# One of the seven block products of layer two's mixing taken as seven smaller ones, with the block sums kept in DRAM

## The chip, the cores and the metric

The kernel runs on one core of a Trainium2 chip. The metric is device time in microseconds (us) for one execution of the whole program: the median of several runs. Profile times are from one profiled execution, counted from the start of its span. The engines are called as the profile calls them: PE (TensorE; PEld is its weight load), DVE (VectorE), ACT (ScalarE), POOL (GpSimd) and SP (SyncE, which issues most DMAs).

## What is computed

Two layers, each a linear-attention block and a mixer block, on 2048 tokens of width 512, all in float32:

```python
def _B_ref(x, w_in, w_sp, b_sp, w_out):
    Fh = F // 2                                   # 896
    z = _gelu(jnp.einsum("bsd,df->bsf", x, w_in))
    z1 = z[..., :Fh]
    z2 = _layernorm(z[..., Fh:], axis=-1)
    g = jnp.einsum("ts,bsf->btf", w_sp, z2) + b_sp[None, :, None]
    return jnp.einsum("bsf,fd->bsd", z1 * g, w_out)

x = A_x
x = x + _A_ref(_layernorm(x, axis=-1), A_wqkv, A_wo)
x = x + _B_ref(_layernorm(x, axis=-1), B_w_in, B_w_sp, B_b_sp, B_w_out)
x = x + _A_ref(_layernorm(x, axis=-1), A_wqkv, A_wo)
x = x + _B_ref(_layernorm(x, axis=-1), B_w_in, B_w_sp, B_b_sp, B_w_out)
```

The weights of both layers are the same arrays. The einsum with `w_sp` (2048 x 2048 times 2048 x 896) is the *mixing*. The change is in the second layer's mixing.

## The kernel before

**Precision.** Every float32 matrix product is made of three: each operand is split into a high part (ScalarE's copy to float32r, `high`, L101) and a low part (VectorE's subtraction, `low`, L104), and TensorE adds high x high, high x low and low x high (`mm3`, L115 to L117; in the mixing L1111 to L1113). So every operand passes through ScalarE and then VectorE before TensorE can use it.

**Order.** The schedule is written out by hand: the order of the calls in the source is the order on each engine's queue, and each queue runs in order. Buffers are numbered slots that are taken and given back in turn: 22 pages of 128x512 (`pg`), 6 quads of 128x2048 (`qd`), 4 big ones (`bg`), and the 8 banks of PSUM. Whoever takes a slot waits until its last user is done.

**Stages of a layer.** (1) Attention, `P1` and `transition`. (2) The projection stage, `P2.run`: a loop over s = 1 to 18, over token blocks of 128. At step s it makes block s - 1's attention output (`c`, 12 matmuls, and `c2`, VectorE's addition to x, L644), its statistics (L222, L224, then three small POOL operations) and its normalised copy (ScalarE, L235), turns that copy by a round through DRAM (`xturn`, VectorE's L286), splits it (`d_high`, `d_low`, L101 and L104 into a `qd`) for block s - 2, multiplies block s - 3 by the second half of `w_in` (`e`, 24 matmuls of 448 columns, deadline of `d_low`), and takes one or two pieces of the first half (`f`, 12 matmuls each). Before `c` it turns and splits the attention operand of block s (`b_high`, `b_low`). The Gelus that empty the banks run on ScalarE (L702, L727). In layer two (`seven` is true) the last 1024 tokens of `f` are made by seven block products (`side`, `tail`), with sums of `w_in` that `Make` made in layer one's output stage and keeps in DRAM (`kept`; POOL's queue fetches them, L774). (3) The mixing, `P4.run`: `w_sp` and z2 are cut in 2 x 2 blocks and multiplied with seven block products instead of eight, in `ORDER`: P4, P2, P1, P6, P7, P5, P3. The tokens are 16 blocks, so each product has 8 steps of 24 or 18 matmuls of 128x512. The sums of `w_sp` blocks that four of the products need were made in layer one by POOL (`Sums`) and are kept in DRAM (`s`). At step g the loop prepares the weights of g + 2 and the z operand of g + 3 (`prepare`: L1070, L1075 on ScalarE, L1077, L1081 on VectorE), issues the matmuls of g (`mm`), and fetches the weights of g + 4 (`fetch`). After a product's last step `evac` adds its banks into `gb`. P2 and P1 of the mixing share the two banks `delta`, which P1 empties. (4) The output stage, in the same `run`: 16 blocks of 21 matmuls with `w_out` (`o`, `zsplit` two blocks ahead, x loaded two blocks ahead, L1212 the addition).

Of the kernel before, what the change touches and what calls it, by code (L numbers as in the profile page):

```python
# [10 lines left out]
F32 = mybir.dt.float32  # L11
# [42 lines left out]
def mixer_kernel(ctx: ExitStack, tc: tile.TileContext, x_in, wqkv, wo_d, win1_d, win2_d, wsp_d, bsp_d, wout_d,  # L54
# [514 lines left out]
    class P2:  # L569
# [309 lines left out]
        def run(self, sums):  # L879
            w1 = self.win1  # L880
            for s in range(1, NT + 3):
                self.loadx(s + 1)
                self.qturn.load(s + 1)
                if s in self.qturn.by_pe:
                    self.c(s - 1)
                    self.b_high(s)
                    self.c2(s - 1)
                    self.b_low(s)
                    self.c_stats(s - 1)
                    if s >= 2:  # L890
# [115 lines left out]
                self.done = [a22, a11, a12]  # L1006


    class P4:


# [2 lines left out]
        WITH3 = ("P4", "P2", "P1", "P5")  # L1014
        H1, H3, H2 = slice(0, 384), slice(384, 512), slice(512, 896)

        def __init__(self, p2, sums):
            self.L = p2.L
            self.p2, self.sums = p2, sums
            self.raw, self.w, self.z, self.z1, self.x, self.zs = {}, {}, {}, {}, {}, {}  # L1020
            self.steps = [(p, k) for p in self.ORDER for k in range(HT)]
            self.beta = self.delta = None
            self.ready, self.loaded = deque(), []
            self.wout = {}

        def fetch(self, g):
            if g >= len(self.steps):
                return
            p, k = self.steps[g]
            t = quads.get([P, 2, 512])  # L1030
            if p in ("P1", "P2", "P4"):
# [32 lines left out]
        def prepare(self, gw, gz):  # L1064

            gw, gz = (g if g is not None and g < len(self.steps) else None for g in (gw, gz))
            if gw is not None:
                r = self.raw.pop(gw)
                w = self.w[gw] = quads.get([P, 2, 2, 512], F32R)
                nc.scalar.activation(w[:, 0], r, AF.Copy)  # L1070
            if gz is not None:
                n = 512 if self.steps[gz][0] in self.WITH3 else 384
                z, sign, t = self.operand(gz)
                h, l = pages.get(PAGE, F32R), pages.get(PAGE, F32R)
                nc.scalar.activation(h[:, 0:n], z, AF.Copy, scale=sign)  # L1075
            if gw is not None:
                nc.vector.tensor_sub(w[:, 1], r, w[:, 0].bitcast(F32))  # L1077
                quads.put(r)
            if gz is not None:
# [7 lines left out]
                self.z[gz] = (h, l)  # L1087

        def mm(self, g):
            p, k = self.steps[g]  # L1090
            h, l = self.z.pop(g)
            w = self.w.pop(g)
            first, last = k == 0, k == HT - 1
            if p in ("P4", "P2", "P5") and first:
                self.delta = [banks.get(PAGE) for _ in range(2)]
            if p in ("P4", "P2", "P1", "P5") and first:
                self.beta = [[banks.get(PAGE) for _ in range(3)] for _ in range(2)]
            if p in self.WITH3:
                for j in range(2):
                    self.acc(self.delta[j], h, l, self.H3, w, j, first and p != "P1",  # L1100
                             last and p != "P2")
# [13 lines left out]
        def unit(self, n, f):  # L1115
            return self.gb[n][:, f, :]
# [24 lines left out]
        def evac(self, p):  # L1141
# [3 lines left out]
            if p in ("P4", "P1", "P5"):  # L1145
                for j in range(2):
                    n = 2 + j if p == "P1" else j
                    V.tensor_add(self.unit(n, 3), self.delta[j], self.unit(n, 3) if p == "P5" else bs[n])
# [70 lines left out]
        def run(self, nxt):  # L1219
# [14 lines left out]
            for g in range(n):  # L1234
# [17 lines left out]
                if k == HT - 1:  # L1252
                    self.evac(p)
            pages.put(*self.bs)
            self.zsplit(1)
# [1 line left out]
            for i in range(NT):  # L1257
                self.loadx(i + 2)
                self.gates()
                if i == NT - 1 and nxt is not None:  # L1260
                    nxt.T(1)
                self.o(i)
                self.zsplit(i + 2)
                if make is not None:
                    make.step(i)
                if nxt is not None:
                    self.join(i, nxt)

# [16 lines left out]
                nxt.T(0)  # L1285

    sums = Sums()
    p1 = P1(0)
    p1.start()
    for L in range(2):  # L1290
# [41 lines left out]
```

## Time and profile before

| what | value |
|---|---|
| median of 3 runs | 1388.9 us (1388.66 to 1390.36) |
| the profiled execution's own time | 1389.01 us |
| its span | 1387.2 us, 17681 instructions |
| PE busy | 1380.8 us, 100%, 6232 matmuls |
| DVE busy | 911.5 us, 66% |
| ACT, POOL busy | 594.3 us (43%), 432.5 us (31%) |
| DMA | 235.67 MB, mean 170 GB/s; 52.4% of 16 engines in the hardware queues, 0.8% in POOL's |

How to read it: the share of busy time is an average over stages. A matmul's listed duration includes the time in which it overlaps with its neighbours; the distance of starts tells what one costs. In a timeline a row has start, duration, engine, line, operation, output<-inputs, and in brackets the idle time before it and what ended that. In this execution layer two's projection stage lies at about 836 to 1020 us, its mixing from 1036 to 1311 us, and layer one's output stage around 620 to 700 us.

### The profile page before, as it was taken

The numbers are of one execution on the slowest core, as the hardware profiler recorded it, in microseconds if no ns is written. First come the engines' busy times: TensorE is split into PE (matmuls) and PEld (weight loads), VectorE is DVE, ScalarE is ACT, GpSimd is POOL, SyncE is SP. The second block draws the span as 40 slices with busy tenths as digits, with TensorE's granted clock in tenths as the row PEclk, the third lists the DMA queues.
The fourth block names the chain that finished last, engine by engine and source line by source line (L and its number), as shares of the span: only waits on it lengthen the run. The fifth ranks groups of instructions, "written<-read, shape, count | busy, mean of one in ns | idle before, by whom it ended". The sixth has DMA issues, their size and how long they took to land.

```text
span 1387.2 us, 17681 instructions
## 1 busy us (share of the span) xinstructions
PE 1380.8 (100%) x6232; PEld 1157.8 (83%) x6232; DVE 911.5 (66%) x1314; ACT 594.3 (43%) x918; POOL 432.5 (31%) x514
## 2 busy tenths in 40 slices
PE   9999999999999999999999999999999999999998
PEld 7888888888888888888888888888888888888887
DVE  6776887753756597676667768866766345776642
ACT  6674543334442234241357655444454432342410
POOL 3343454443135451432023425522220000233310
PEclk9999999999999999999999999999999999999999
DMA  5541367866678974356845415555364324544442
GB/s 172 174 129 62 118 186 229 258 207 212 217 242 287 296 236 134 126 205 229 279 130 162 128 46 152 175 175 162 120 212 148 103 91 129 175 129 159 167 145 91
DMA packets 151145, 235.67 MB, mean 170 GB/s; under 512 B 12560, under 2 KB 56592, under 8 KB 151056
## 3 DMA queue, kind: packets, MB, share of 16 engines
q1 hardware_dynamic: 147456, 228.11, 51.3%
q0 software_dynamic: 1728, 3.15, 0.8%
q10 hardware_dynamic: 1872, 3.28, 0.6%
q8 instruction: 49, 0.80, 0.2%
q14 instruction: 40, 0.33, 0.1%
HBM read 162.40 MB, written 72.09 MB: 169 GB/s over the span
## 4 chain that ended last, share of the span: by engine, by line
PE 99%; DMA 0%; DVE 0%; POOL 0%; ACT 0%; issue 0%; DVEq 0%
PE bank L117 19%; PE bank L115 19%; PE bank L116 19%; PE bank L1112 13%; PE bank L1113 13%; PE bank L1111 13%; PE bank L793 1%; PE bank L794 1%; PE bank L792 1%; PE bank L247 1%; DMA pg<-in_x_dram 0%; DVE st L222 0%; ACT pg L101 0%; POOL rs L227 0%; DVE pg L237 0%; PE bank L516 0%
## 5 line engine op out<-in xcount | busy, mean ns | idle before, releaser
L1112 PE MATMUL bank<-qd,pg 128*128 128x512 f32 x800 | 311.3, 389 | 0.0
L1111 PE MATMUL bank<-qd,pg 128*128 128x512 f32 x800 | 311.2, 389 | 0.0
L1113 PE MATMUL bank<-qd,pg 128*128 128x512 f32 x800 | 311.2, 389 | 0.0
L1077 DVE TENSOR_TENSOR qd<-qd,qd 128x1024 fp32r<-128x1024 f32 x112 | 160.4, 1432 | 143.5 <-ACT qd L1070 143.0
L1070 ACT ACTIVATE qd<-qd 128x1024 fp32r<-128x1024 f32 x112 | 118.6, 1059 | 241.4 <-DMA qd<-s 109.6
L1133 POOL TENSOR_TENSOR bg<-bg,pg 128x512 f32<-128x512 f32 x56 | 81.4, 1458 | 320.8 <-DMA pg<-z 294.9
L1112 PEld LDWEIGHTS bank<-qd,pg 128*128 128x128 f32 x800 | 150.2, 188 | 31.5 <-DVE qd L1077 0.4
L1111 PEld LDWEIGHTS bank<-qd,pg 128*128 128x128 f32 x800 | 150.2, 188 | 31.4
L1113 PEld LDWEIGHTS bank<-qd,pg 128*128 128x128 f32 x800 | 150.2, 188 | 31.0
L117 PE MATMUL bank<-qd,pg 128*128 128x512 f32 x384 | 149.9, 390 | 0.0
L226 POOL TENSOR_SCALAR rs<-mv 128x1 f32<-128x1 f32 x96 | 39.1, 407 | 332.7 <-DVE mv L224 332.4
L986 POOL TENSOR_TENSOR pg<-pg,pg 128x512 f32<-128x512 f32 x64 | 92.5, 1445 | 91.0 <-DMA pg<-in_wsp_dram 65.1
L235 ACT ACTIVATE pg<-pg,nb,rs 128x512 f32<-128x512 f32 x63 | 51.1, 811 | 145.7 <-POOL nb L229 145.4
L115 PE MATMUL bank<-qd,pg 128*128 128x512 f32 x288 | 112.4, 390 | 0.1
L116 PE MATMUL bank<-qd,pg 128*128 128x512 f32 x288 | 112.1, 389 | 0.0
L115 PE MATMUL bank<-bg,qd 128*128 128x448 f32 x256 | 94.0, 367 | 0.0
L116 PE MATMUL bank<-bg,qd 128*128 128x448 f32 x256 | 93.6, 366 | 0.0
L117 PE MATMUL bank<-bg,qd 128*128 128x448 f32 x256 | 93.4, 365 | 0.0
L101 ACT ACTIVATE pg<-pg 128x512 fp32r<-128x512 f32 (+1 forms) x87 | 53.5, 615 | 81.2 <-DVE pg L286 38.0
L286 DVE STREAM_TRANSPOSE pg<-pg 128x512 f32<-128x512 f32 x79 | 85.1, 1077 | 4.5 <-DMA pg<-yt 1.7
L115 PE MATMUL bank<-wo,qd 128*128 128x512 f32 x224 | 87.1, 389 | 0.0
L116 PE MATMUL bank<-wo,qd 128*128 128x512 f32 x224 | 87.1, 389 | 0.0
(157 smaller groups left out, 2683.2 us busy)
## 6 DMA issues: line engine op xcount, KB each, us to landing
qd<-s SPq DMA_DIRECT2D x64, 512.0 KB, 3.4
qd<-in_wsp_dram SPq DMA_DIRECT2D x48, 512.0 KB, 4.3
pg<-in_wsp_dram SPq DMA_DIRECT2D x64, 256.0 KB, 4.9
s<-pg SPq DMA_DIRECT2D x64, 256.0 KB, 4.8
pg<-x SPq DMA_DIRECT2D x64, 256.0 KB, 3.3
pg<-z SPq DMA_DIRECT2D x56, 256.0 KB, 3.8
x<-pg SPq DMA_DIRECT2D x48, 256.0 KB, 2.9
z<-pg SPq DMA_DIRECT2D x44, 256.0 KB, 2.1
```

The source lines that it names most:

```text
L101: nc.scalar.activation(h, src, AF.Copy)
L115: nc.tensor.matmul(out, ah, bh, start=start, stop=False)
L116: nc.tensor.matmul(out, ah, bl, start=False, stop=False)
L117: nc.tensor.matmul(out, al, bh, start=False, stop=stop)
L286: nc.vector.transpose(y.rearrange("p c (t m) -> p m c t", m=4), r.rearrange("p (m c j) -> p m c j", m=4, c=4))
L986: nc.gpsimd.tensor_tensor(t, a, b, op=OP.add)
L1070: nc.scalar.activation(w[:, 0], r, AF.Copy)
L1077: nc.vector.tensor_sub(w[:, 1], r, w[:, 0].bitcast(F32))
L1111: m(out, h[:, o], w[:, 0, j, :], start=start, stop=False, skip_group_check=True)
L1112: m(out, h[:, o], w[:, 1, j, :], start=False, stop=False, skip_group_check=True)
L1113: m(out, l[:, o], w[:, 0, j, :], start=False, stop=stop, skip_group_check=True)
L1133: nc.gpsimd.tensor_tensor(u, u, z1, op=OP.mult)
```

## The change

In layer two's mixing, the product P2 (blocks a = `w_sp` rows of the third and fourth quarter, columns of the second half; z operand the second half of the tokens, first 512 features) is itself cut in 2 x 2 blocks and taken with seven products, in the order `NEST`. Its 8 steps of 24 matmuls become 14 steps ("N", two to a product) of 12 matmuls of 128x512. Three of the seven use blocks of `w_sp` that are loaded and split as before; four use sums, which a new class `Inner` makes once, splits, and keeps in DRAM as ready high and low parts; POOL's queue fetches these, 1 MB for a step. `Inner` makes 16 sums, each a *unit*: one addition or subtraction on VectorE, a high part on ScalarE, a low part on VectorE, and in the next unit two stores of 256 KB by SP. Four units run in layer one's output stage, twelve in layer two's projection stage. The z operands need sums as well (`token_sums`, in P4's steps; four pages held until P5). The inner products gather in banks X (two, over P1, P6, P7, P4, read out after each) and Y (two, for P2, P3, P5 each), and are added into `gb` on VectorE after each. Since the 128 features of `delta` are now done with the others, P1 of the outer product starts its own `delta` bank and adds into `gb`.

The core of the diff:

```diff
@@ P2.run
                 if self.seven:
                     self.side(s)
+                    if s == 5:
+                        inner.begin(3)
+                    elif 6 <= s < 16:
+                        for _ in range(2 if 10 <= s < 13 else 1):
+                            inner.unit()
...
+    class Inner:
+        def __init__(self):
+            self.d = {m: dram.tile([2, P, 2, 2, 512], F32, name=f"n{m}") for m in range(1, 5)}
...
+        def store(self):
+            for m, k, n, p in self.made:
+                nc.sync.dma_start(self.d[m][k // 2][:, k % 2, n, :], p.bitcast(F32))
+                pages.put(p)
+            self.made = []
+
+        def unit(self):
+            self.store()
+            if not self.todo:
+                return
+            k, u = self.todo.popleft()
+            if u == 0:
+                self.S1 = t = self.raw.pop("22")
+                nc.vector.tensor_add(t, self.raw["21"], t)
+            elif u == 1:
+                t = self.raw.pop("21")
+                nc.vector.tensor_sub(t, self.raw["11"], t)
...
+            h, l = pages.get(PAGE, F32R), pages.get(PAGE, F32R)
+            split(h, l, t)
...
+            if self.left:
+                self.fetch()
+                self.left -= 1
...
     class P4:
+        NEST = ("P1", "P6", "P2", "P7", "P3", "P4", "P5")
+        OWN = {"P1": (2, 8), "P2": (2, 12), "P4": (3, 12)}
+        SUM = {"P3": 4, "P5": 1, "P6": 2, "P7": 3}
...
+            for p in self.ORDER:
+                if p == "P2" and self.nested:
+                    self.steps += [("N", d) for d in range(14)]
+                else:
+                    self.steps += [(p, k) for k in range(HT)]
...
     def fetch(self, g):
+            if p == "N" and self.NEST[k // 2] in self.SUM:
+                self.w[g] = quads.get([P, 2, 2, 512], F32R)
+                nc.gpsimd.dma_start(self.w[g], inner.d[self.SUM[self.NEST[k // 2]]][k % 2])
+                return
...
+        def token_sums(self, k):
+            q, o = divmod(k, 2)
+            if o == 0:
+                self.T2[q], self.T3[q] = pages.get([P, 2, 256]), pages.get([P, 2, 256])
+            a, b = ztile[8 + k], ztile[12 + k]
+            nc.vector.tensor_sub(self.T3[q][:, o], b[:, 256:512], a[:, 256:512])
+            nc.vector.tensor_add(self.T2[q][:, o], self.T3[q][:, o], a[:, 0:256])
...
+        def nested_mm(self, g):
...
+            for i in range(2):
+                f = slice(i * P, (i + 1) * P)
+                for o in range(2):
+                    first, last = q == 0 and o == 0, q == 1 and o == 1
+                    m(out[i], h[:, o, f], w[:, o, 0], start=first and (own or name == "P1"), stop=False,
+                      skip_group_check=True)
+                    m(out[i], h[:, o, f], w[:, o, 1], start=False, stop=False, skip_group_check=True)
+                    m(out[i], l[:, o, f], w[:, o, 0], start=False, stop=last and (own or name == "P4"),
+                      skip_group_check=True)
...
+                if name == "P1":
+                    V.tensor_add(u[1], self.X[i], bs[2])
+                elif name == "P6":
+                    V.tensor_add(u[2], self.X[i], bs[2])
+                elif name == "P2":
+                    V.tensor_add(u[1], u[1], self.Y[i])
...
@@ P4.run
+                if self.nested and 1 <= g < 5:
+                    self.token_sums(g - 1)
...
                 if make is not None:
                     make.step(i)
+                    if i < 5:
+                        inner.unit() if i else inner.begin(1)
+                    elif i == 5:
+                        inner.store()
```

More of the change, by code (lines that the diff above doesn't have):

```diff
@@ L1020, in __init__ @@
             self.raw, self.w, self.z, self.z1, self.x, self.zs = {}, {}, {}, {}, {}, {}
-            self.steps = [(p, k) for p in self.ORDER for k in range(HT)]
+            self.nested = p2.seven
+            self.steps = []
+            for p in self.ORDER:
+                if p == "P2" and self.nested:
+                    self.steps += [("N", d) for d in range(14)]
+                else:
+                    self.steps += [(p, k) for k in range(HT)]
+            self.T2, self.T3 = {}, {}
             self.beta = self.delta = None
@@ L1066, in prepare @@
             gw, gz = (g if g is not None and g < len(self.steps) else None for g in (gw, gz))
+            if gw is not None and gw not in self.raw:
+                gw = None
             if gw is not None:
@@ L1069, in prepare @@
                 w = self.w[gw] = quads.get([P, 2, 2, 512], F32R)
-                nc.scalar.activation(w[:, 0], r, AF.Copy)
-            if gz is not None:
+                wh, wl = (w[:, :, i] if self.steps[gw][0] == "N" else w[:, i] for i in range(2))
+                nc.scalar.activation(wh, r, AF.Copy)
+            inside = gz is not None and self.steps[gz][0] == "N"
+            if inside:
+                self.nested_high(gz)
+            elif gz is not None:
                 n = 512 if self.steps[gz][0] in self.WITH3 else 384
@@ L1076, in prepare @@
             if gw is not None:
[L1077 removed]
+                nc.vector.tensor_sub(wl, r, wh.bitcast(F32))
                 quads.put(r)
[L1079 removed]
+            if inside:
+                self.nested_low(gz)
+            elif gz is not None:
                 if sign > 0:
@@ new lines, in nested_high, with nested_low @@
+        def nested_high(self, g):
+            _, _, src = self.nested_operand(g)
+            h, l = self.z[g] = pages.get([P, 2, 256], F32R), pages.get([P, 2, 256], F32R)
+            if isinstance(src, list):
+                for o in range(2):
+                    high(h[:, o], src[o])
+            else:
+                high(h, src)
+        def nested_low(self, g):
+            name, q, src = self.nested_operand(g)
+            h, l = self.z[g]
+            if isinstance(src, list):
+                for o in range(2):
+                    low(l[:, o], src[o], h[:, o])
+                return
+            low(l, src, h)
+            for o in range(2):
+                a, b = ztile[8 + 2 * q + o], ztile[12 + 2 * q + o]
+                if name == "P6":
+                    nc.vector.tensor_sub(src[:, o], b[:, 0:256], src[:, o])
+                elif name == "P7":
+                    nc.vector.tensor_sub(src[:, o], a[:, 256:512], a[:, 0:256])
+            if name in ("P4", "P5"):
+                pages.put(src)
@@ new lines, in nested_mm @@
+        def nested_mm(self, g):
+            name, q = self.NEST[self.steps[g][1] // 2], self.steps[g][1] % 2
+            h, l = self.z.pop(g)
+            w = self.w.pop(g)
+            if q == 0:
+                if name == "P1":
+                    self.X = [banks.get(PAGE) for _ in range(2)]
+                elif name in ("P2", "P3", "P5"):
+                    self.Y = [banks.get(PAGE) for _ in range(2)]
+            own = name in ("P2", "P3", "P5")
+            out = self.Y if own else self.X
+            m = nc.tensor.matmul
+            for i in range(2):
+                f = slice(i * P, (i + 1) * P)
+                for o in range(2):
+                    first, last = q == 0 and o == 0, q == 1 and o == 1
[4 more added lines that the diff above has]
+                      skip_group_check=True)
+            pages.put(h, l)
+            quads.put(w)
+            if q == 0:
+                return
+            V, bs = nc.vector, self.bs
+            for i in range(2):
+                u = {n: [self.unit(2, i), self.unit(2, 2 + i), self.unit(3, i), self.unit(3, 2 + i)][n - 1]
+                     for n in range(1, 5)}
+                if name == "P1":
+                    V.tensor_add(u[1], self.X[i], bs[2])
[3 more added lines that the diff above has]
+                    V.tensor_add(u[1], u[1], self.Y[i])
+                elif name == "P7":
+                    V.tensor_add(u[4], self.X[i], bs[3])
+                elif name == "P3":
+                    V.tensor_add(u[2], u[2], self.Y[i])
+                elif name == "P4":
+                    V.tensor_add(u[3], self.X[i], bs[3])
+                else:
+                    V.tensor_add(u[4], u[4], self.Y[i])
+                    V.tensor_add(u[2], u[2], self.Y[i])
+                if own:
+                    banks.put(self.Y[i])
+                elif name == "P4":
+                    banks.put(self.X[i])
@@ L1093, in mm @@
             first, last = k == 0, k == HT - 1
-            if p in ("P4", "P2", "P5") and first:
+            if (p in ("P4", "P2", "P5") or p == "P1" and self.nested) and first:
                 self.delta = [banks.get(PAGE) for _ in range(2)]
@@ L1099, in mm @@
                 for j in range(2):
-                    self.acc(self.delta[j], h, l, self.H3, w, j, first and p != "P1",
+                    self.acc(self.delta[j], h, l, self.H3, w, j, first and (p != "P1" or self.nested),
                              last and p != "P2")
@@ L1147, in evac @@
                     n = 2 + j if p == "P1" else j
-                    V.tensor_add(self.unit(n, 3), self.delta[j], self.unit(n, 3) if p == "P5" else bs[n])
+                    held = p == "P5" or p == "P1" and self.nested
+                    V.tensor_add(self.unit(n, 3), self.delta[j], self.unit(n, 3) if held else bs[n])
                     if p != "P4":
@@ L1251, in run @@
                         self.zsplit(0)
-                if k == HT - 1:
+                if p != "N" and k == HT - 1:
                     self.evac(p)
@@ L1287, in mixer_kernel @@
     sums = Sums()
+    inner = Inner()
     p1 = P1(0)
```

41 lines of the change are left out of this document (40 added, 1 removed).

## The prediction

> **What bounds the kernel now.** I read the page first, then who waited for whom on TensorE, then single matmuls, and last VectorE's timeline in the stages that receive new work. The page says that TensorE is the kernel:
>
> ```profile
> PE 1380.8 (100%) x6232; PEld 1157.8 (83%) x6232; DVE 911.5 (66%) x1314; ACT 594.3 (43%) x918; POOL 432.5 (31%) x514
> PE 99%; DMA 0%; DVE 0%; POOL 0%; ACT 0%; issue 0%; DVEq 0%
> ```
>
> All of TensorE's waits in the whole execution, by the answer for that engine:
>
> ```profile
> PE bank L434 <- DVE pg L429: 2.3, 1, 2.3
> PE bank L247 <- DVE pg L237: 0.3, 1, 0.3
> ```
>
> Both lie in the first 8 us. So a matmul removed is time gained, and any delay elsewhere is free until it uses up the lead that an operand has over its matmul, and is then paid in full. The page's 389 ns of a matmul is not its price, because matmuls overlap. The mixing's timeline gives the price by the distance of starts:
>
> ```profile
> 1119.08 0.39 PE L1112 MATMUL bank<-qd,pg 128*128 128x512 f32 x1
> 1119.31 0.39 PE L1113 MATMUL bank<-qd,pg 128*128 128x512 f32 x1
> 1119.53 0.39 PE L1111 MATMUL bank<-qd,pg 128*128 128x512 f32 x1
> ```
>
> From 1118.63 to 1122.93 there are 19 starts: 0.2266 us each.
>
> **Part 1, the product itself.** P2 of layer two was 8 steps of 24 matmuls (192); it becomes 14 steps of 12 (168), all still 128x512. The programs' instruction lists agree: 24 fewer. 24 x 0.2266 = 5.4 us off the path. [...]
>
> **Part 2, making the sums.** Sixteen units: VectorE add or subtract, ScalarE high part, VectorE low part, two stores. Four fall in layer one's output stage (i = 1 to 4), twelve in layer two's projection stage: one behind each of steps s = 6 to 9, two behind 10, 11, 12, one behind 13 and 14. No matmul needs them soon, yet they sit in the same in-order queues as operands that are needed. The low part waits for ScalarE, and everything of the next step on VectorE stands behind it. One unit thus costs VectorE 0.69 + 0.62 + 0.69 (rows of a 128x512 tensor_tensor, of L101 and of L104) and two hand-offs of 0.03 (ScalarE's L101 at 945.60 ends 946.22, VectorE's L104 starts 946.25): 2.06 us. How much room is there? VectorE in this stage:
>
> ```profile
> 946.25 0.69 DVE L104 TENSOR_TENSOR pg<-pg,pg 128x512 fp32r<-128x512 f32 x1 [1.81 <-ACT pg L101]
> 947.83 0.69 DVE L644 TENSOR_TENSOR pg<-pg,bank 128x512 f32<-128x512 f32 x1 [0.88 <-PE bank L117]
> 952.54 0.69 DVE L104 TENSOR_TENSOR qd<-pg,qd 128x512 fp32r<-128x512 f32 x1 [1.50 <-ACT qd L101]
> 953.99 1.15 DVE L222 BATCH_NORM_STATS2 st<-z_z 128x6 f32<-128x448 f32 x2 [0.76 <-ACT z_z L702]
> 965.59 0.69 DVE L104 TENSOR_TENSOR qd<-pg,qd 128x512 fp32r<-128x512 f32 x1 [1.50 <-ACT qd L101]
> ```
>
> A step lasts 13.05 us (60 matmuls) and VectorE idles 1.81 + 0.88 before c2's add (L644): 2.7 us that a delay can eat. The 1.50 is not free: it is the chain add, statistics, POOL, normalise, high part, and moves with the add. The second L104 is d_low, which ends block k's operand; TensorE's first 448-column matmul of the block is its deadline. The lead, by subtracting d_low's end from that start, is 6.8 us for block 5 (891.34 to 898.13), 7.4, 7.5, 7.4 for 8 to 10, then 4.7 (966.28 to 971.01), 3.6, 4.3, 2.2 (995.71 to 997.93) and 4.1 for 11 to 15: steps 13 to 17 are shorter (10.3, 9.0, 10.3, 7.6, 9.0).
>
> Now add up VectorE's delay D at step s (block s - 2). A single unit costs its 2.06 even in a 13-us step, because its ScalarE half queues behind the same Gelu that ends the 1.81 idle; but it does not accumulate there, so D = 2.1 up to s = 9. Step 10 follows a 10.3-us step and has no idle before c2 (its L644 starts at 921.72 without a wait): D = 2.1 + 2.1 = 4.1. Step 11: + two units 4.1, - idle 2.7 = 5.5. Step 12: 6.9. Step 13: + 4.1 - (2.7 + the 0.76 before L222) = 7.5, against a lead of 4.7. Step 14: + 2.1 - (0.37 + 0.76) = 8.4 against 3.6. Step 15: + 2.1 - 0.76 = 9.7 against 4.3. Step 16: - 0.34 = 9.4 against 2.2: TensorE has by then lost **7.2 us**, and step 17 adds none. [...] I take 7.2, since the chain is read from neighbouring rows of the same stage.
>
> The stage's added transfers (36 of 256 KB, 9.4 MB in about 100 us, 94 GB/s on 161 to 183) on shares of 0.50 to 0.58 leave the DMA engines between 80 and 90% busy; nothing here, and in rival (d) what it costs if that is too little.
>
> In layer one's output stage the four units cost 8 us of VectorE in 19 us, where 10-us stretches show 4.9 to 8.3 us busy and an operand is made two steps (9.5 us) ahead: nothing. Their 12 transfers (3.1 MB) are another matter. The stretches from 630 to 680 us show DMA shares of 0.67, 0.70, 0.98, 0.69 and 0.97, with 331 GB/s at 0.98, so 3.1 MB is 9.4 us of full engines; some 6 fit into the first two, the rest pushes loads of x back. L1212 already waits 0.75 for x at 680.38. Between 0 and 3 us; I take 1.0, as the next thin stretch takes the backlog.
>
> **Part 3, the nested steps.** Four of the seven inner products get ready parts and need no split of weights; three still split theirs. VectorE in the 14 x 2.72 = 38.1 us of TensorE: 6 low parts at 1.14, 14 operand low parts at about 0.68, 8 half-page subtractions at 0.42 and 16 additions at 0.69: 30.8 us, 81%. The new wait: P6 continues in X while P1's sum is read out of it, so the first P6 matmul waits for a VectorE add (0.69). X[0] is complete half a step (1.36 us) earlier, so the add fits if VectorE is at hand; a low part ahead of it could hold it 1.2 us. P1 to P6 is the only hand-over of X from one step to the next; the other two have a pair of steps between. 0 to 4 (all three, and the stage's start), and 0.3 taken. POOL's eight 1 MB loads: a 256 KB one lands in 4.2 us (POOL's row for the kept sums; 3.1 to 8.3), the software queue moved 3.15 MB in 0.8% of the span (11.1 us), so 1 MB takes about 4.2 + 2.8 = 7.0 us; the fetch is four steps ahead, 10.9 us. POOL has nothing else queued there (0.00 busy from 1047 to 1121). Hidden, with 3.9 us to spare. Token sums (8 half-page operations) and the moved `delta` start in P1 lie in idle VectorE time of P4: nothing.
>
> **Sum.** On the profiled execution's own 1389.0 us (span 1387.2 and 1.8 around it; the median is 1388.9, the same within 0.1): - 5.4 + 7.2 + 1.0 + 0.3 = + 3.1, so 1392.1, and **1392.0** on the median. What a measurement can tell from no change is about 0.2%, 2.8 us.
>
> **Rivals.** (a) *The units fit, faster.* If ScalarE and VectorE fill each other's waits, a unit costs 1.4 us. Then D is 1.4, 2.7 at step 10, about 2.7 at 11 and 12, 2 at 13, 2.3 at 14, 2.9 at 15, 2.6 at 16: only the last touches a lead, by 0.4. Time 1389.0 - 5.4 + 0.4 to 1.4: 1384 to 1385. For it: VectorE is idle 28% of 866 to 970. Against: the queue is in order and the low part cannot move past. Decided at about 1.6 us a unit. Chance 0.16. (b) *Forecast's kind:* the lag costs 3 to 9; 0.66. (c) *POOL's loads come late, slower.* From a landing above 10.9 us each of eight nested steps waits; at 12 us that is 1.1 x 8 = 9 us more, 1401. For it: one 256 KB landing of 8.3. Against: median 4.2. Chance 0.07. [...] (d) *Loads in a full DMA stage, slower:* output-stage backlog 3 and late x and turned tiles in the projection stage another 3: 1397 to 1398; 0.11. That the count of matmuls does not fall is excluded by the lists.
>
> **How the numbers follow.** Slower by over 0.2%: 0.38 of (b), (c) and (d): 0.56. Within: 0.27, nearly all from (b). Faster: (a) and a sliver of (b): 0.17. Range: from (a)'s upper end, 1385, to 1399, which holds (d) and the full bounds of part 2, and leaves out (a)'s core and (c).
>
> **What would show it.** TensorE waits for ScalarE L101 or VectorE L104 within about 975 to 1015, at the first 448-column matmul of blocks 11 to 14, summing to 3 to 9 us; none at all there would refute part 2. d_low of block 8 about 4 us later than 927.13. 6208 matmuls, and 168 of them in a nested stage of 38 us; a longer stage, or TensorE waiting for POOL's loads, would refute part 3. Waits for L104 at `o` in layer one near 660 to 690 would be the full DMA.

## The result: 0.4% slower, and the profile after

| what | before | after |
|---|---|---|
| median | 1388.78 us (1388.64 to 1390.36, 4 runs) | 1394.97 us (1394.65 to 1395.96, 4 runs) |
| the profiled execution's own time, and its span | 1389.01 us, 1387.2 us | 1395.96 us, 1394.2 us |

The ratio of after to before is 1.0041, interval 1.0029 to 1.0053: slower by 6.2 us of the medians. The profiled execution of after is its longest one, 1.0 us above the median; most of that lies in the first 20 us, as shown below. One execution of the kernel before (5828.9 us) and one of the kernel of experiment 5 (4155.36 us) were slow, far outside all others, and stand in no median or ratio here. The page of after, its line of engines and the chain that ended last:

```profile
PE 1380.3 (99%) x6208; PEld 1154.0 (83%) x6208; DVE 942.1 (68%) x1382; ACT 605.2 (43%) x944; POOL 442.6 (32%) x522
PE 90%; DVE 4%; DMA 2%; ACT 2%; issue 1%; POOL 1%; SPq 0%; ACTq 0%; DVEq 0%; POOLq 0%
```

The count of matmuls fell by 24 as the change says, and the chain, which before was 99% TensorE, now leaves it for a tenth of the span. All of TensorE's waits (total, times, longest):

```profile
PE bank L115 <- ACT qd L101: 4.4, 4, 2.0
PE bank L434 <- DVE pg L429: 2.3, 1, 2.3
PE bank L115 <- ACT pg L101: 1.5, 1, 1.5
PE bank L117 <- DVE qd L104: 0.5, 1, 0.5
PE bank L1303 <- DVE qd L1168: 0.4, 1, 0.4
PE bank L247 <- DVE pg L237: 0.3, 1, 0.3
PE bank L792 <- DMA pg<-win_sums: 0.2, 1, 0.2
PE bank L117 <- DVE pg L104: 0.2, 1, 0.2
```

Of the lines that are new the first is the largest: the operand that meets `w_in` in layer two's projection stage comes late. Waits do not add up to the loss, because the matmuls behind a wait start at wider spacing (0.31, 0.42 and 0.31 us behind block 11's wait, where 0.20 is usual). So I compare when the same matmul starts in both traces. The differences, after minus before:

| place | shift reached | added here |
|---|---|---|
| layer one's 448-column block 4 (196.35 to 197.95) | 1.60 | 1.60, the start |
| layer two's first 448-column block (847.98 to 850.36) | 2.38 | 0.78, layer one's output stage |
| its block 15 (1006.91 to 1018.21) | 11.30 | 8.92, layer two's projection stage |
| the mixing's first matmul (1034.92 to 1046.77) | 11.85 | 0.55, a late load at L792 |
| the output stage's last L115 (1382.72 to 1389.56) | 6.84 | -5.01, mixing and output |

Within the projection stage the shift stays at 2.38 up to block 10 and is then 5.16, 7.77, 9.16, 10.78 and 11.30 for blocks 11 to 15. In the mixing one matmul (L1303 at 1058.49, in the third step of its first product, P4) starts 0.81 behind the one before it instead of 0.23, so the product itself gave 5.01 + 0.58 = 5.59 us. The 168 matmuls of the nested steps run from 1091.04 to 1128.89, 0.2267 us each at a granted clock of 1.00, and none of them waits.

A second profile of after, taken beside experiments 4 and 5 (1395.18 us), has 0.77 at the start and 0.23 in the output stage in place of 1.60 and 0.78, but 9.05 in the projection stage. The first two move from run to run; the third does not.

### The profile page after: what moved, and what is told of

Read it like the earlier page. It is cut to its first block, busy times and chain, and to the rows that moved or that the text cites. A ratio compares the mean times of both kernels' runs of the same rounds, so it can differ in the third digit from the quotient of the medians.

```text
span 1394.2 us, 17840 instructions
## 1 busy us (share of the span) xinstructions
PE 1380.3 (99%) x6208; PEld 1154.0 (83%) x6208; DVE 942.1 (68%) x1382; ACT 605.2 (43%) x944; POOL 442.6 (32%) x522
## 2 busy tenths in 40 slices
DMA packets 158667, 255.60 MB, mean 183 GB/s; under 512 B 13424, under 2 KB 57456, under 8 KB 157552
## 4 chain that ended last, share of the span: by engine, by line
PE 90%; DVE 4%; DMA 2%; ACT 2%; issue 1%; POOL 1%; SPq 0%; ACTq 0%; DVEq 0%; POOLq 0%
PE bank L117 17%; PE bank L115 17%; PE bank L116 17%; PE bank L1303 12%; PE bank L1304 12%; PE bank L1302 12%; PE bank L1247 1%; PE bank L1244 1%; PE bank L1246 1%; DVE st L222 1%; PE bank L247 1%; ACT pg L101 0%; DVE qd L104 0%; DMA pg<-win_sums 0%; DMA pg<-z 0%
## 5 line engine op out<-in xcount | busy, mean ns | idle before, releaser
L1303 PE MATMUL bank<-qd,pg 128*128 128x512 f32 x736 | 286.4, 389 | 0.4 <-DVE qd L1168 0.4
L1302 PE MATMUL bank<-qd,pg 128*128 128x512 f32 x736 | 286.3, 389 | 0.0
L1304 PE MATMUL bank<-qd,pg 128*128 128x512 f32 x736 | 286.3, 389 | 0.0
L1168 DVE TENSOR_TENSOR qd<-qd,qd 128x1024 fp32r<-128x1024 f32 x110 | 157.5, 1432 | 116.4 <-ACT qd L1158 116.0
L1303 PEld LDWEIGHTS bank<-qd,pg 128*128 128x128 f32 x736 | 138.2, 188 | 29.5 <-DVE qd L1168 0.8
L1302 PEld LDWEIGHTS bank<-qd,pg 128*128 128x128 f32 x736 | 138.2, 188 | 28.9 <-DVE pg L854 0.2
L1304 PEld LDWEIGHTS bank<-qd,pg 128*128 128x128 f32 x736 | 138.2, 188 | 28.4
L117 PE MATMUL bank<-qd,pg 128*128 128x512 f32 x384 | 150.4, 392 | 0.2 <-DVE pg L104 0.2
L101 ACT ACTIVATE pg<-pg 128x512 fp32r<-128x512 f32 (+1 forms) x111 | 68.1, 617 | 108.9 <-DVE pg L286 52.4
L115 PE MATMUL bank<-qd,pg 128*128 128x512 f32 x288 | 113.1, 393 | 1.5 <-ACT pg L101 1.5
L116 PE MATMUL bank<-qd,pg 128*128 128x512 f32 x288 | 112.6, 391 | 0.0
L115 PE MATMUL bank<-bg,qd 128*128 128x448 f32 x256 | 95.1, 372 | 4.4 <-ACT qd L101 4.4
L104 DVE TENSOR_TENSOR pg<-pg,pg 128x512 fp32r<-128x512 f32 (+1 forms) x109 | 77.2, 711 | 26.7 <-ACT pg L101 24.8
L117 PE MATMUL bank<-wo,qd 128*128 128x512 f32 x224 | 87.2, 389 | 0.5 <-DVE qd L104 0.5
```

The source lines that it names most:

```text
L104: nc.vector.tensor_sub(l, src, h.bitcast(F32))
L115: nc.tensor.matmul(out, ah, bh, start=start, stop=False)
L116: nc.tensor.matmul(out, ah, bl, start=False, stop=False)
L117: nc.tensor.matmul(out, al, bh, start=False, stop=stop)
L1168: nc.vector.tensor_sub(wl, r, wh.bitcast(F32))
L1302: m(out, h[:, o], w[:, 0, j, :], start=start, stop=False, skip_group_check=True)
```

## Experiments

The theory under test was the forecast's: a unit delays VectorE's in-order queue, and the delay reaches TensorE in the short last steps of the projection stage. Its rivals were the added transfers, and the nested product.

**1. The transfers alone.** All loads, all 32 stores and the nested product stay; the additions and splits of the units go, and the loaded block is stored in their place.

```diff
-                self.S1 = t = self.raw.pop("22")
-                nc.vector.tensor_add(t, self.raw["21"], t)
...
-            split(h, l, t)
+            p = self.raw.pop(("22", "21", "11", "12")[u])
+            self.made = [(m, k, 0, p), (m, k, 1, p)]
```

> The changed kernel with the sixteen units reduced to their transfers: every load and every store of 256 KB stays, a loaded page is stored as it is, and the additions, high parts and low parts of the units are left out (so the ready parts hold the wrong numbers; the nested steps run as before the cut). Theory V (VectorE's and ScalarE's queues are late because a unit stands in them): the projection stage of layer two loses nothing, block 15's first 448-column matmul comes back from 1018.2 to about 1008 to 1010 us, and the time is the kernel before minus 5.4 plus 0 to 2: 1383.5 to 1386. Theory D (the transfers make x and turned tiles late): most of the loss stays, 1391 or more.

Measured: 1384.52 us (1383.81 to 1385.65), ratio 0.9966, interval 0.9954 to 0.9977, where before was 1389.01 beside it. TensorE's waits in this kernel:

```profile
PE bank L434 <- DVE pg L429: 2.3, 1, 2.3
PE bank L115 <- ACT pg L101: 1.1, 1, 1.1
```

Both are in the first 9 us. Block 15 of the projection stage starts at 1006.90, before's was 1006.91, and from the mixing's first matmul to the output stage's last L115 this kernel takes 5.58 us less than before. So the transfers (255.59 MB in all, in after 255.60), POOL's eight loads and the nested product cost nothing that shows, the product brings 5.6, and the whole loss belongs to the units' work on VectorE and ScalarE, or to the pages that this work holds: a block that is only loaded and stored needs none for a high and a low part, so this run does not separate the two. The 0.58 at L1303 in the mixing of after and its late load at L792 do not occur here either.

**2. The units alone.** The sums are made and stored as in the change, but P2 stays as it was.

```diff
-            self.nested = p2.seven
+            self.nested = False
```

> The sixteen units where the change has them, but the mixing without the nested product (its eight steps of 24 matmuls as before). Theory V: the loss of the projection stage (8.9 us between blocks 0 and 15 in the changed kernel's profile) stays whole and nothing is gained: 1389 + 8.9 + about 0.7 for the output stage = 1397 to 1400. Theory N (the nested stage costs what was not gained, by its new waits): 1389 to 1392.

Measured: 1400.71 us (1400.34 to 1400.93), ratio 1.0084, interval 1.0068 to 1.0099, a little above what was expected. Against the changed kernel that is 5.7 more, the product's 5.6 again. The projection stage loses 9.5 us here, 8.9 to 9.05 in the changed kernel. The mixing loses 1.3 us as well, in the first steps of P4, where TensorE waits 0.4 us at L1303 for L1168 as in the changed kernel. Nothing is nested here, so that wait belongs to the units and not to the nested product.

**3. The same units, one behind each step from 4 to 15.** Four still lie in layer one's output stage. The unit itself is unchanged.

```diff
-                    if s == 5:
-                        inner.begin(3)
-                    elif 6 <= s < 16:
-                        for _ in range(2 if 10 <= s < 13 else 1):
-                            inner.unit()
+                if self.L == 1:
+                    if s == 3:
+                        inner.begin(3)
+                    elif 4 <= s < 17:
+                        inner.unit()
```

> The changed kernel with one unit behind each of steps 4 to 15, in place of one or two behind 6 to 14; the unit is unchanged. Theory V: the delay does not pile up over steps 10 to 13 (about 2 to 3 us at step 13 in place of 7.5), so blocks 11 to 13 no longer wait, but units behind steps 14 and 15 fall where the lead is 2.2: a loss of 4 to 6 us, 1388 to 1391. Theory D: the same bytes in the same stage, 1394 to 1396.

Measured: 1395.91 us (1395.59 to 1396.31), ratio 1.0049, interval 1.0034 to 1.0064. That is where the transfers' theory wanted it, and my expectation missed. But experiment 1 had taken the transfers' side away, so I looked for what I had misjudged. The waits are of the known kind and larger:

```profile
PE bank L115 <- ACT qd L101: 6.7, 4, 3.9
```

I had thought that the doubled units of steps 10 to 12 were the harm. The trace says that any such unit in a late step is. VectorE's `d_low` is 5.4 us late already at block 4, where the units meet the busy 8-us steps and VectorE once waits 2.59 us for a page whose store is under way, stays between 5.7 and 8.6 through the long steps, and is then 7.3, 9.3 and 11.8 late at blocks 12, 13 and 14. VectorE in one of the late steps:

```profile
983.79 0.69 DVE L104 TENSOR_TENSOR qd<-pg,qd 128x512 fp32r<-128x512 f32 x1 [1.80 <-ACT qd L101]
985.25 1.15 DVE L222 BATCH_NORM_STATS2 st<-z_z 128x6 f32<-128x448 f32 x2 [0.76 <-ACT z_z L702]
986.50 0.21 DVE L224 BATCH_NORM_AGGREGATE mv<-st 128x2 f32<-128x12 f32 x1
986.63 0.64 DVE L1053 TENSOR_TENSOR pg<-pg,pg 128x512 f32<-128x512 f32 x1
988.03 0.69 DVE L104 TENSOR_TENSOR pg<-pg,pg 128x512 fp32r<-128x512 f32 x1 [0.76 <-ACT pg L101]
988.64 1.08 DVE L286 STREAM_TRANSPOSE pg<-pg 128x512 f32<-128x512 f32 x1
```

The unit is the fourth and fifth row. From the addition's start to the next operation's start it takes 2.01 us, 0.76 of it idle, waiting for its own high part. Nothing in the step gives that back: the 0.76 and 1.80 in front of the other rows are VectorE's own results on their way through ScalarE and POOL, and they move with it.

**4. The same steps, the low part one unit later.** Against experiment 3 the unit is changed: a low part is made by the next unit, when the high part is long done (in every second unit over the sum's own page), and loads are one unit ahead instead of two.

```diff
+        def finish(self):
+            for m, k, u, h, t, old in self.pend:
+                ...
+                    low(l, t, h)
...
-            split(h, l, t)
+            h = pages.get(PAGE, F32R)
+            high(h, t)
+            self.pend.append(((1, 3, 2, 4)[u], k, u, h, t, old))
...
-            self.fetch()
-            self.fetch()
-            self.left = 4 * n - 2
+            self.fetch()
+            self.left = 4 * n - 1
```

> The same places as one unit behind each of steps 4 to 15, but a unit's low part is made by the next unit, one step later, so that VectorE no longer waits inside the unit for ScalarE's high part (and loads are one unit ahead instead of two, since a page is held longer). The forecast's mechanism says that the price of a unit on VectorE's queue falls from about 2.06 us to about 1.4 us, so that the short late steps (10.3, 9.0, 10.3, 7.6 us) hold it: 1386 to 1390 us, and at most 3 us lost in the projection stage instead of 11.4. The rival that only the amount of work counts (the same additions, high and low parts and stores on the same engines in the same steps) says no change from that kernel: 1395 to 1396.5 us, and TensorE waits for ScalarE L101 of 5 to 7 us.

Measured: 1387.65 us (1386.86 to 1388.56, 11 runs), ratio 0.9992, interval 0.9983 to 1.0000, where before was 1388.9 beside it. The same additions, high parts, low parts and stores in the same steps, and 8.3 us less than experiment 3. TensorE's waits for the operand fall from 6.7 us to this:

```profile
PE bank L115 <- ACT qd L101: 0.3, 1, 0.3
```

VectorE's unit becomes the first two of these rows:

```profile
969.93 0.64 DVE L104 TENSOR_TENSOR pg<-pg,pg 128x512 fp32r<-128x512 f32 x1
970.49 0.69 DVE L1070 TENSOR_TENSOR pg<-pg,pg 128x512 f32<-128x512 f32 x1
971.09 1.09 DVE L286 STREAM_TRANSPOSE pg<-pg 128x512 f32<-128x512 f32 x1
```

Neither has an idle time. From the low part's start to the next operation's start it is 1.16 us, 0.85 less than above. `d_low` of block 14 is 3.3 us late instead of 11.8, and the stage loses 0.8 us up to block 15 instead of 11.4.

But two things changed at once: pages are held differently too, and the 2.59 us for a page are 0.26 here. So the loads' share was taken alone: **experiment 3 with loads one unit ahead**, the last part of the diff above and nothing else.

> One unchanged unit behind each of steps 4 to 15, as in the kernel that took 1395.9 us, but with loads one unit ahead instead of two, so that one page fewer is held. That is the one other difference between that kernel and the one with the low part one unit later (1387.65 us). In the first, VectorE once waits 2.59 us for a page whose store is under way. If the 8.3 us between them are the low part's wait inside the unit, this kernel stays at 1393 to 1396.5 us. If they are waits for pages, it falls to 1387 to 1390 us. Between the two, up to 2.6 us may belong to the pages.

Measured: 1394.84 us (1393.92 to 1395.55, 5 runs), ratio 1.0040, interval 1.0026 to 1.0054, its before 1388.85. VectorE's wait for a page in the stage is down from 2.59 to 0.87 us (ScalarE waits once, 1.1 us, in layer one's output stage), and yet TensorE waits almost as long:

```profile
PE bank L115 <- ACT qd L101: 5.3, 3, 4.0
```

`d_low` of blocks 11 to 14 is 3.5, 5.1, 7.0 and 9.5 us late, against 0.6, 1.3, 2.5 and 3.3 with the low part later. So of the 8.3 us some 1.1 may belong to pages and loads (two sets of runs, whose intervals overlap), and 7.2 to the wait inside the unit, because it stands in VectorE's queue. The unit's own handling of pages differs too between these two kernels; with 0.87 us waited for them it can be no large part. Some 2.4 us of the 7.2 come on top of the wait, an estimate from the starts behind it (experiment 5): with loads one ahead, fourteen matmuls of block 14 start 0.37 us apart instead of 0.204, with the low part later none; the mean granted clock of the two profiles is 0.997 and 1.000. The amount of work does not decide.

**5. Matmuls in the wait.** In the first trace of after, the granted clock falls behind the first 2-us wait (2.02 us, up to 976.17), to a mean of 0.90 and 0.93 in these windows:

```profile
970.00:980.00 10.00, 7.75 (x29) 5.58 (x28) 7.12 (x14) 4.73 (x8) 2.09 (x5) 0.90 0.67 184
980.00:990.00 10.00, 9.45 (x40) 7.67 (x39) 6.33 (x10) 4.48 (x8) 2.05 (x5) 0.93 0.59 197
```

(The columns behind the five engines are the clock, the DMA share and GB/s.) Single matmuls show it too:

```profile
976.17 0.47 PE L115 MATMUL bank<-bg,qd 128*128 128x448 f32 x1 [2.02 <-ACT qd L101]
...
978.41 0.58 PE L117 MATMUL bank<-bg,qd 128*128 128x448 f32 x1
978.78 0.58 PE L115 MATMUL bank<-bg,qd 128*128 128x448 f32 x1
979.16 0.58 PE L116 MATMUL bank<-bg,qd 128*128 128x448 f32 x1
...
987.76 0.47 PE L115 MATMUL bank<-bg,qd 128*128 128x448 f32 x1 [0.49 <-ACT qd L101]
```

The slow ones start 0.373 us apart instead of 0.204. I thought that this explained why the stage loses more than its waits, some 1.5 us of the 8.9. So ten matmuls of 448 columns that no result uses were put ahead of block 11's:

```diff
+                if self.L == 1 and i == 11 and j == 0:
+                    for _ in range(10):
+                        nc.tensor.matmul(b, w.h[:, 0, 0:128], w.h[:, 0, 0:448], start=True, stop=True)
```

> The changed kernel with ten matmuls of 448 columns more, of no use to the result, ahead of block 11's first 448-column matmul: 10 x 0.204 = 2.04 us of work in the place of the 2.02 us wait. If the granted clock fell because TensorE stood idle, the nine matmuls at 0.375 us there go back to 0.204 and the restart is smooth: the time falls by 1.5 to 2 us below the changed kernel's, to about 1393.0 to 1393.5, with a granted clock of 1.00 from 970 to 990. If the clock fell for another reason, the matmuls only fill the wait: no change, 1394.5 to 1395.5, or up to 2 us more if they delay the block.

> The changed kernel as it is, beside the other three on the same chip: 1394.5 to 1396 us, with the wait of about 2 us ahead of block 11 and some nine matmuls of 448 columns at 0.375 us behind it in both theories.

Measured: 1395.26 us (1394.64 to 1397.36) with them and 1395.18 (1394.14 to 1396.79) without, ratios to before 1.0047 (1.0034 to 1.0060) and 1.0047 (1.0035 to 1.0059). No gain. The clock did stay up in the wait that was filled, and fell behind the next instead; but in the second profile of after it also stayed up there, behind a wait of 2.00 us that nothing filled. Windows of the kernel with the matmuls, from 970 and from 990 us:

```profile
970.00:980.00 10.00, 9.46 (x41) 7.02 (x40) 7.61 (x14) 4.33 (x7) 1.33 (x3) 1.00 0.71 214
990.00:1000.00 10.00, 10.00 (x41) 8.73 (x41) 6.80 (x11) 3.23 (x6) 2.79 (x6) 0.83 0.38 115
```

Why it gains nothing is read from the starts of blocks 11 and 12. In the first profile of after they are 11.59 us apart, with slow matmuls between; in the second 11.58, with all 24 matmuls of block 11 at 0.20 to 0.21 us behind the first few; with the ten matmuls 11.57. VectorE's round of a step sets this distance (next section), and a slower TensorE only waits less at its end. Where the fall came behind block 12 instead (second profile, and with the matmuls), block 13 does start later, 12.37 and 12.32 us behind block 12 instead of 11.72; but block 14 waits again in all three, and lies 20.94, 20.96 and 20.96 us behind block 12. My reading of the clock as a part of the loss is refuted for this kernel.

Behind the last late block no wait follows that could take it up. Experiment 3's trace shows that there it does cost: the granted clock is 0.50 from 1006.13 to 1012.96, twelve matmuls of block 14 start 0.37 us apart, some 2.0 us more than at 0.204, and from block 14 to block 15 it takes 11.46 us, before 8.98.

**6. Versions without the harm.** Both have the low part one unit later. One has four units in layer one's projection stage (steps 4 to 7), four in its output stage and eight in layer two's projection stage, in steps 4 to 11 alone. The other has none in the output stage, and twelve in layer two's steps 4 to 15.

```diff
+                if self.L == 0:
+                    if s == 3:
+                        inner.begin(1)
+                    elif 4 <= s < 10:
+                        inner.unit([1, 1, 1, 1, 0, 0][s - 4])
```

> Units in which VectorE makes the low part one unit later, when ScalarE's high part is long there, and none behind a step later than 11: four behind steps 4 to 7 of layer one's projection stage, four in its output stage, eight behind steps 4 to 11 of layer two's projection stage. Theory V: a unit costs VectorE 1.4 us and no wait, eight do not use up the leads of 6 to 7 us, and the time is 1389 - 5.4 + 0 to 2: 1383.5 to 1386, below both kernels. Theory D: bytes as before, 1391 or more.

Measured: 1385.57 us (1385.10 to 1387.45, 10 runs), ratio 0.9977, interval 0.9967 to 0.9986. The projection stage loses 0.1 us up to block 15. What is left of TensorE's waits outside the first 9 us is in layer one's output stage:

```profile
PE bank L117 <- DVE qd L104: 0.6, 2, 0.4
```

> A further version: low parts one unit later, four units in layer one's projection stage (steps 4 to 7) and twelve in layer two's (steps 4 to 15), none in layer one's output stage. It differs from the kernel with low parts one unit later only in where the first four units lie. If the four units in the output stage cost what the forecast gave them (1.0 us, full DMA), it is 0.5 to 1 us below that kernel; if they cost nothing, it is the same within 0.5. In either theory it is under 1390 if the price of the low part's wait decides, and 1394 or more if only the amount of work counts.

Measured: 1386.42 us (1385.80 to 1388.19, 11 runs), ratio 0.9984, interval 0.9976 to 0.9993; 1.2 us below experiment 4, which ran beside it. In its trace nothing is added in layer one's output stage (847.98 becomes 847.99), in experiment 4's 1.13 us and in the first version's 1.28. Both versions are faster than both kernels; between the two the intervals overlap.

Is it the places or the unit that makes the first version fast? It was run with the unchanged unit, loads two ahead, in its places:

> The unchanged unit, with its wait for the high part, at the places of the fastest version: four behind steps 4 to 7 of layer one's projection stage, four in its output stage, eight behind steps 4 to 11 of layer two's projection stage (loads two ahead). If units hurt only because of the short steps from 12 on, this is as fast as that version, 1385 to 1387 us, and the wait in the unit has no price here. If the wait in the unit decides wherever it stands, each unit still leaves VectorE some 0.8 us later, the delay at block 11 is 4 to 7 us against a lead of 4.7, the late steps give back less than 1 us, and it is 1387.5 to 1391 us.

Measured: 1392.21 us (1390.53 to 1394.08, 10 runs), ratio 1.0020, interval 1.0011 to 1.0029: above what either theory said. The trace has no loss at all behind block 8, where no unit stands any more and the shift is 8.32 throughout, but 3.8 us ahead of the stage and 4.1 at its blocks 5 to 8. VectorE has a long wait of the same kind in each layer's projection stage, 3.20 us in layer one, and in layer two this one, with another of 1.10 behind it:

```profile
883.84 0.69 DVE L104 TENSOR_TENSOR pg<-pg,pg 128x512 fp32r<-128x512 f32 x1 [3.18 <-DMA n<-pg]
```

VectorE waits for a page that SP's queue is still storing. That was in neither theory: the places free the late steps, as the first said, but the unit holds several of the 22 pages, and where steps are short and full its pages come back too late. This run does not separate the loads two ahead from the wait for the high part.

## Why the prediction was right, and where its sum was off

**The side and the place** were right: slower, by waits at L115 for ScalarE L101, at the first 448-column matmul of blocks 11 to 14, between 976 and 1009 us, 4.4 us of them. The median lies 3.0 us above the forecast, the profile 3.7 above the terms forecast for it; 1.7 of that belong to the projection stage, and 2.7 to three terms that the sum did not have. On the terms, by the first profile:

| term | predicted | measured |
|---|---|---|
| the product | -5.4 | -5.59 |
| units in the projection stage | +7.2 | +8.92 (second profile 9.05) |
| units in layer one's output stage | +1.0 | +0.78 (second profile 0.23) |
| nested steps | +0.3 | 0 |
| late load before the mixing | 0 | +0.55 (second profile 1.10) |
| wait at L1303 in the mixing's first product | 0 | +0.58 (second profile 0.51) |
| the start, which the change does not touch | 0 | +1.60 (second profile 0.77) |

**The mis-sized term is the projection stage.** The delay of `d_low` behind before's, less the 2.38 with which the stage starts:

| step | 9 | 10 | 11 | 12 | 13 | 14 | 15 | 16 |
|---|---|---|---|---|---|---|---|---|
| predicted | 2.1 | 4.1 | 5.5 | 6.9 | 7.5 | 8.4 | 9.7 | 9.4 |
| measured | 1.7 | 3.5 | 4.6 | 7.2 | 8.2 | 9.7 | 11.7 | 11.3 |

The price of a unit was right: 2.06 predicted, and in the trace of after 978.92 to 980.87, 1.95. Up to step 11 the table is 0.9 above the trace. Two steps of it failed after that. First, at steps 13, 14 and 15 I counted the 0.76 us of idle ahead of the statistics (L222) as room that a delay eats. Here are the same rows of after, by which time VectorE is 8 to 10 us late:

```profile
976.15 0.69 DVE L104 TENSOR_TENSOR qd<-pg,qd 128x512 fp32r<-128x512 f32 x1 [1.51 <-ACT qd L101]
977.61 1.15 DVE L222 BATCH_NORM_STATS2 st<-z_z 128x6 f32<-128x448 f32 x2 [0.76 <-ACT z_z L702]
978.92 0.64 DVE L1052 TENSOR_TENSOR pg<-pg,pg 128x512 f32<-128x512 f32 x1
980.26 0.69 DVE L104 TENSOR_TENSOR pg<-pg,pg 128x512 fp32r<-128x512 f32 x1 [0.70 <-ACT pg L101]
980.87 1.09 DVE L286 STREAM_TRANSPOSE pg<-pg 128x512 f32<-128x512 f32 x1
...
983.32 0.68 DVE L644 TENSOR_TENSOR pg<-pg,bank 128x512 f32<-128x512 f32 x1
...
987.74 0.69 DVE L104 TENSOR_TENSOR qd<-pg,qd 128x512 fp32r<-128x512 f32 x1 [1.83 <-ACT qd L101]
989.20 1.16 DVE L222 BATCH_NORM_STATS2 st<-z_z 128x6 f32<-128x448 f32 x2 [0.76 <-ACT z_z L702]
```

The 0.76 is still there. ScalarE reaches the Gelu (L702) only after the high part and the normalising that VectorE's own late chain releases, so this idle moves with the delay, as the 1.5 in front of `d_low` does, which the forecast did treat so. The idle ahead of c2's addition (L644), which waits for TensorE, is eaten as assumed: its row has none. So is the 1.81 ahead of `b_low` in a 13-us step (at 970.91 it is gone), although its releaser reads L101 too: in the trace of before that high part stands behind a Gelu which itself waited 2.12 us for TensorE's bank (L727 at 945.11). Three times 0.76 is 2.3; the measured rise over these steps is 1.7 more than the predicted one.

Second, the table had no term for pages. Behind step 11 two units run, and in step 12 VectorE waits for a page of the unit before them: the first of the two issued its store at 949.72, and it landed at 954.68:

```profile
954.76 1.10 DVE L286 STREAM_TRANSPOSE pg<-pg 128x512 f32<-128x512 f32 x1 [1.37 <-DMA n<-pg]
```

With it the delay grows by 2.55 us at step 12 instead of the 1.4 predicted. Together, -0.9 + 1.15 + 1.7 makes 11.3 of the 9.4, and 11.3 less the lead of 2.2 is 9.1, the 8.9 of the trace. VectorE's round, from one `d_low` to the next, is 976.15 to 987.74, 11.59 us, where TensorE before needed 9.0 from block 11 to 12 and 10.3 from 12 to 13: the loss grows in every late step, and a filled wait changes nothing. The 9 us up to which the forecast lets the lag rise was an estimate for units slowed by POOL's work beside them. The trace of before has one such row (L104 at 897.33, 1.37 us instead of 0.69, beside POOL's L109 from 896.86 to 898.15), the trace of after none in the units: between 866 and 1010 us their additions, subtractions and low parts (L1046, L1049, L1052, L1056, L104) take 0.63 to 0.69 us.

**The output stage**: the size holds but its reason falls. I put 1.0 there for full DMA engines. Experiment 1 has the same transfers and loses nothing there; the waits are for VectorE's L104, whose slack of two steps I had counted as enough. The nine traces with units there lose 0.2 to 1.3 us.

**The nested steps**: the 0.3 taken was for X, and X costs nothing; VectorE is busy for 26.62 of 38.09 us there, 70% where I had added up 81%. The one new wait of the mixing, at L1303 for VectorE's L1168, lies ahead of the nested steps, in P4. Experiment 2 has it without a nested product and experiment 1, with one, does not, so it is a late effect of the units, for which the sum had no term. Of the rivals, (c) is refuted, since nobody on TensorE waits for POOL's loads. In the median they land sooner than the 7.0 us that I had estimated, and the slowest two, 7.2 and 9.1 us, still within the 10.9 of the four steps ahead:

```profile
qd<-n POOLq DMA_DIRECT2D x8, 1024.0 KB, 5.9
```

(d) is refuted by experiment 1. (a) was wrong for this unit, but it named the point from which it decides, some 1.6 us a unit, and the kernels with one unit behind each of steps 4 to 15 lie on both sides of it: at 2.0 us 1394.8 to 1395.9, at 1.2 us 1387.7.

**Outside the sum**: the start was not in it, rightly so. Its shift belongs to the run: in the first profile TensorE waited 1.54 us at 8.74 and the granted clock was 0.50 from 8.61 to 12.02, in the second it waited 1.00 us and the clock stayed at 1.00. The kernel of experiment 4 starts 0.14 us ahead of before's profile, that of experiment 1 with it, and the two profiles of after differ by 0.8.

## What to carry to other kernels

Before filling an engine's idle time with new work, ask of each idle stretch what ends it: one that ends on another engine's own pace (here TensorE's bank, L644) is room, one that ends on the echo of this engine's earlier result (here L101, L702) moves with the delay and is none. The releaser's line alone does not tell them apart (L101 ends both kinds here), so follow it back to what that engine waited for. Put no wait for another engine inside the filler: making the low part one unit later, on finished inputs, was worth 7 us with the same work in the same places. Count the buffers that the filler holds until its stores are done, too. And put the filler where the bounding engine's steps are long; steps shorter than the filled engine's round lose the difference every time (here 9.0 and 10.3 us against 11.59).

## What the runs showed of the hardware

In the first profile of after the granted clock was 0.50 from 977.99 to 981.40, behind a wait of 2.02 us that ended at 976.17: about nine matmuls of 448 columns at 0.373 us instead of 0.204. It does not fall each time; in the second profile of after a wait of 2.00 us was followed by 20 matmuls at 0.20 to 0.21 us, and the fall came behind the next one, of 1.72 us. The fall lasts 3.41 and 3.42 us, here in the first and the second profile:

```profile
977.99:981.40 3.41, 3.41 (x11) 3.03 (x11) 2.68 (x6) 1.13 (x3) 1.74 (x3) 0.50 0.66 202
987.30:990.72 3.42, 3.39 (x9) 3.06 (x10) 1.92 (x4) 2.25 (x5) 0.98 (x2) 0.50 0.44 110
```

Six traces have a fall in layer two (both of after, experiments 2, 3 and 5, and the one with loads one ahead); the mean granted clock of these profiles is 0.997 to 0.999. In experiment 3 it lasts 6.83 us (1006.13 to 1012.96). So in these traces the length of a wait does not decide alone whether a fall follows: 1.72 us had one behind it, and 2.00 us had none.
